# Another order of the work inside a turn: both later score tiles right behind the largest, two copies exchanged between the engines

## The chip, the cores and the metric

The kernel runs on one core of a Trainium2 chip. The core has four engines that compute, each with an instruction queue of its own: TensorE (PE in the profile, with its weight loads as PEld), VectorE (DVE), ScalarE (ACT) and GpSimd (POOL). SyncE (SP) and POOL issue the transfers. The engines wait for each other on semaphores. The metric is the device time of one execution in microseconds (us); the median of three runs of the kernel before is 439.67 us (438.95 to 440.5).

## The reference

Causal attention in blocks, and then a mixture of experts on its output:

```
scores = q @ k^T / 8            # 8 batches, 8 heads, 576 positions, 64 columns
scores = where(block(i) >= block(j), scores, -1e9)      # blocks of 64
attn   = exp(scores - max) / (sum + 1e-9);   x = attn @ v      # x: 4608 x 512
logits = x @ w_gate;  expert = argmax;  gate = softmax weight of that expert
for each of 8 experts: the 80 tokens of the highest gate
    out[tok] = gate * (relu(x[tok] @ w1[e]) @ w2[e])
```

All other rows of the output are zero.

## The kernel before, in words

Attention works on 32 pairs: pair i is batch i // 4 and two of its heads. For a pair, the 576 query rows are cut into five tiles. Tile u (0 to 3) has 128 rows, and because of the blocks its scores are (u + 1) * 128 + 64 columns wide: 192, 320, 448 and 576. Tile 4 is the first 64 rows, 64 columns. Each tile exists for both heads, h = 0 and 1. The steps of a pair, by their names in the table that orders them:

- `prep` 0 and 1: q and k, loaded in pieces, are turned by VectorE (L527); POOL scales the turned q (L530).
- `scores`: "3" makes tile 3 (a PSUM buffer for each head), "2" makes tiles 2 and 4 in one buffer, "10" makes tiles 1 and 0 in one buffer (L547, with the masking product L554).
- `max`: VectorE's negated maximum of each row (L583), for one head or for both.
- `soft`: ScalarE's exponential of a tile and head from PSUM into the array P, with the row's sum (L592).
- `back`: TensorE turns P in blocks of 64, "B" from tiles 1 and 2, "A" from tile 3, "C" the rest (L620, L628), each into one PSUM buffer.
- `take back`: a copy of that buffer to SBUF, A and B into PT, C into PF (L675 on ScalarE, L677 on VectorE; the dictionary TAKE says which).
- `values` 0 and 1: the product with v (L667, L646), from PT and PF into one PSUM buffer; `take values` copies it to xT, and `flip` turns it for the store (L294).
- `gate`: after the fourth pair of a batch, the parts of the routing: the sums' reciprocals (`recip`), the logits (`logits0`, their copy `lgc0` at L325, their turning `lt`, scaling `lm` at L351 and L360), the softmax (`ga`, `gexp`, `gb`), and its rearranging (`gturn`, `turn2`, `wcopy`).

All these PSUM buffers come from one pool of four (`ps_a`, L271), each of two banks, so that they hold the whole PSUM. A step that asks for a buffer gets one whose last reader stands earlier in the program, and waits for that reader. Five kinds of step ask: "3" for two, "2", "10", each `back` and `values` for one, and `logits0`, `lt` and `turn2` for one.

The order is written out by hand. In turn i (the loop at L702, from -5 to 37) the kernel goes through the table TURN; an entry (d, step, ...) does the step for pair i + d. No scheduler changes it: each engine gets its own instructions in the order in which the steps stand in the table. So TURN decides, for every engine, what stands in front of a waiting instruction, and for every PSUM buffer whom it waits for. A gate part of offset d falls into one turn of every four.

After the last pair come the selection of tokens and the experts' products, whose weights are streamed from HBM; this part has no line that the change touches.

Of the kernel before, what the change touches and what calls it, by code (L numbers as in the profile page):

```python
# [27 lines left out]

NVZ = 3

TAKE = {"back": {"A": "a", "B": "v", "C": "a"}, "values": {0: "a"}}

TWICE = (2,)

TURN = (
    (0, "scores", "3"),
    (-1, "take", "back", "C"),
    (0, "soft", 0, 1),
    (0, "max", 3, 1),
    (1, "begin"),  # L40
    (1, "scores", "2"),
    (0, "soft", 1, 0),
    (0, "soft", 0, 0),
    (0, "max", 3, 0),
    (1, "max", 2, 1),
    (0, "soft", 3, 1),
    (1, "max", 4),
    (1, "max", 2, 0),
    (-3, "gate", "ga"),
    (-1, "values", 0),  # L50
    (0, "soft", 3, 0),
    (0, "soft", 1, 1),
    (-1, "values", 1),
    (1, "soft", 2, 0),
    (-1, "gate", "recip"),
    (-5, "gate", "turn2"),
    (2, "prep", 0),
    (-2, "gate", "logits0"),
    (-5, "gate", "wcopy"),
    (0, "back", "B"),  # L60
    (1, "load_v"),
    (1, "soft", 4, 0),
    (-1, "take", "values", 0),
    (-4, "gate", "gb"),
    (1, "soft", 2, 1),
    (-2, "gate", "lgc0"),
    (1, "soft", 4, 1),
    (0, "back", "A"),
    (2, "prep", 1),
    (5, "load"),  # L70
    (-2, "gate", "lt"),
    (0, "take", "back", "B"),
    (1, "scores", "10"),
    (-4, "gate", "gturn"),
    (-2, "gate", "lm"),
    (0, "back", "C"),
    (1, "max", 0),
    (0, "take", "back", "A"),
    (1, "max", 1),
    (-2, "flip"),  # L80
    (-3, "gate", "gexp"),
)


# [1 line left out]
def tile_attn_moe(ctx, tc, q, k, v, w_gate, w1, w2, capacity, out, xs=None, dbg=None):  # L86
    nc = tc.nc
    B, H, S, D = q.shape
# [67 lines left out]
    def clear(i):  # L156
        if ov is not None:
            if 0 <= i < nz:
                nc.gpsimd.dma_start(ov[i], zero.unsqueeze(1).broadcast_to([P, 2, DM]))
        elif i == 0:  # L160
            for j in range(NTOK // BLK):
                nc.sync.dma_start(out[j * BLK:(j + 1) * BLK, :], zero[0:BLK, 0:DM])
# [30 lines left out]
    def constants():  # L193
        nc.gpsimd.memset(dl, 1e-9)
        nc.gpsimd.memset(zero, 0.0)
        nc.gpsimd.iota(iota_e, pattern=[[1, E]], base=-E, channel_multiplier=0,
                       allow_small_or_imprecise_dtypes=True)
        nc.gpsimd.iota(iota_v, pattern=[[0, NT], [1, E]], base=-E, channel_multiplier=0,
                       allow_small_or_imprecise_dtypes=True)
        nc.gpsimd.memset(iota_v[BLK:P, NT - 1], 64.0)  # L200
        nc.gpsimd.memset(prod[:, NT - 1], 0.0)

    def constants2():

        nc.vector.tensor_reduce(sameE, ident.rearrange("p (e j) -> p e j", j=16), axis=AX.X, op=ALU.add)
        nc.gpsimd.memset(sameR3, 0.0)
        nc.vector.tensor_reduce(sameR, ident.rearrange("p (e j) -> p j e", j=16), axis=AX.X, op=ALU.add)
        nc.gpsimd.tensor_copy(same.rearrange("p (e j) -> p e j", j=16), sameE.unsqueeze(2).broadcast_to([P, E, 16]))
        nc.gpsimd.memset(ones, 1.0)
        nc.gpsimd.iota(iota_s, pattern=[[1, CHUNK]], base=0, channel_multiplier=0,  # L210
                       allow_small_or_imprecise_dtypes=True)
        for i in range(2):
            nc.gpsimd.iota(iota_b[:, i], pattern=[[1 + i, CHUNK]], base=0, channel_multiplier=0,
                           allow_small_or_imprecise_dtypes=True)
        nc.gpsimd.iota(iota_p, pattern=[[0, 1]], base=0, channel_multiplier=1, allow_small_or_imprecise_dtypes=True)

        nc.gpsimd.affine_select(out=before, in_=same, compare_op=ALU.is_gt, fill=0.0, base=0,
                                pattern=[[1, P]], channel_multiplier=-1)
        nc.gpsimd.affine_select(out=after, in_=same, compare_op=ALU.is_gt, fill=0.0, base=0,
                                pattern=[[-1, P]], channel_multiplier=1)  # L220
        nc.gpsimd.tensor_tensor(before1, before, ident, op=ALU.add)
        nc.gpsimd.tensor_tensor(after1, after, ident, op=ALU.add)
        nc.gpsimd.iota(iota_c, pattern=[[1, 16]], base=0, channel_multiplier=0,
                       allow_small_or_imprecise_dtypes=True)

    def capacities():
        nc.vector.tensor_tensor(iota_c16, sameR, iota_c, op=ALU.mult)
        nc.vector.tensor_reduce(iota_r, iota_c16, axis=AX.X, op=ALU.add)
        nc.gpsimd.tensor_copy(cf, ci)
        nc.vector.scalar_tensor_tensor(cap, cf[:, 1:2], 4294967296.0, cf[:, 0:1], op0=ALU.mult, op1=ALU.add)  # L230
        nc.vector.tensor_tensor(caplt, iota_p, cap, op=ALU.is_lt)
# [41 lines left out]
    def banks():  # L273
        return ps_a.tile([P, 2, 512], F32, name="sc")
# [187 lines left out]
    class Pair:  # L462
# [209 lines left out]
        def take(self, what, x):  # L672

            if TAKE[what][x] == "a":
                nc.scalar.copy(*self.out.pop((what, x)))  # L675
# [3 lines left out]
    def warm(n, wt, after=None, w=identr, c=4):  # L679

        if not n:
            return
        with ExitStack() as order:
            if after is not None:
                order.enter_context(tc.issue_after(after.ins))
            for i in range(n):
                nc.tensor.matmul(wt[:, 0:c * P].rearrange("p (a c) -> p a c", c=P), lhsT=w,
                                 rhs=w.unsqueeze(1).broadcast_to([P, c, P]), start=(i == 0), stop=(i == n - 1))
# [9 lines left out]
    with tc.manual_schedule():  # L698
        warm(WARM[0], banks()[:, 0], w=idle)
        constants()  # L700
        constants2()
        for i in range(-5, n + 6):  # L702
            if i == -1:
                nc.sync.dma_start(ci, capacity.bitcast(U32).partition_broadcast(P))
                for h in range(2):
                    nc.sync.dma_start(wgd[h * D:(h + 1) * D, :, h * E:(h + 1) * E], wg_v[h])

            if i >= 4 and (i % 2 or i % 8 == 4) and i < n:
                clear(cleared)
                cleared += 1  # L710
            if i == 5:
                capacities()
            if n - 3 <= i < n - 3 + FW0:
                weights(1)
            for d, what, *args in (TURN if i != -1 else sorted(TURN, key=lambda x: x[1] == "prep")):
                j = i + d
                if not 0 <= j < n:
                    continue
                if what == "gate":
                    if j % NP == NP - 1 and j < n - 1:  # L720
                        batches[j // NP].part(args[0])
                    continue
                if what == "flip" and j >= n - NP:
                    continue
                getattr(pairs[j], what)(*args)
                if what == "flip" and j % NP == NP - 1:
                    batches[j // NP].done()
                if what == "take" and args[0] == "values" and j >= n - NP:
                    pairs[j].flip()
                    pairs[j].bt.store_pair(pairs[j].pr)  # L730
            if i == n:
                batches[B - 1].recip()
                batches[B - 1].store(False)
        while cleared < nz:
            clear(cleared)
            cleared += 1
        bt = batches[B - 1]
        for part in ((0, 384), (384, S)):
            bt.logits((part,))
            bt.lgc()  # L740
        bt.logits2(0, (3, NT))
        bt.logits2(1, (3, NT))
        bt.gate()
        bt.turn(nc.vector, 2)
        bt.turn2()
# [29 lines left out]
    key = sel.tile([P, 2, NH], F32, name="key")  # L775
# [503 lines left out]
```

## Time and profile before

| | us |
|---|---|
| median of three runs | 439.67 (438.95 to 440.5) |
| the profiled execution's own time | 436.93 |
| its span, first to last instruction | 434.9 |
| the first `values` of the program start at | 22.49 |
| the last `values` of the last pair start at | 307.33 |

The profile's page gives the busy time of each engine, the span in 40 slices, and the costliest groups of instructions. A row of the timeline gives the start of a group of like instructions, its length, the engine, the line, what it writes and reads, how many there are, and in brackets how long the engine stood idle before it and what ended that. The length of a group of TensorE is modelled to the end of its last instruction; the next group can start before that.

### The profile page before, as it was taken

The numbers are of one execution on the slowest core, as the hardware profiler recorded it, in microseconds if no ns is written. First come the engines' busy times: TensorE is split into PE (matmuls) and PEld (weight loads), VectorE is DVE, ScalarE is ACT, GpSimd is POOL, SyncE is SP. The second block draws the span as 40 slices with busy tenths as digits, with TensorE's granted clock in tenths as the row PEclk, the third lists the DMA queues.
The fourth block names the chain that finished last, engine by engine and source line by source line (L and its number), as shares of the span: only waits on it lengthen the run. The fifth ranks groups of instructions, "written<-read, shape, count | busy, mean of one in ns | idle before, by whom it ended". The sixth has DMA issues, their size and how long they took to land. (4 is left out here: it accounts for less than half of the span.)

```text
span 434.9 us, 15422 instructions
## 1 busy us (share of the span) xinstructions
PE 378.2 (87%) x6322; PEld 311.3 (72%) x6322; DVE 282.8 (65%) x586; ACT 265.0 (61%) x797; POOL 180.2 (41%) x296
## 2 busy tenths in 40 slices
PE   8789989899899889999989899899684999998990
PEld 4467767677777777777767677767463999998890
DVE  5987878987887897788789789885552221111121
ACT  2987878887887887798798878878320211110000
POOL 6535554443664445366344636562146400000010
PEclk9999999999999999999999999999988899999996
DMA  8999999989999898999989989399979999998920
GB/s 139 147 154 134 190 193 169 190 159 147 210 187 179 168 182 159 160 204 190 170 174 174 170 154 203 130 300 347 355 138 280 296 310 327 325 316 304 316 93 21
DMA packets 203836, 88.78 MB, mean 204 GB/s; under 512 B 168701, under 2 KB 185853, under 8 KB 203760
## 3 DMA queue, kind: packets, MB, share of 16 engines
q1 hardware_dynamic: 190112, 53.37, 63.0%
q0 software_dynamic: 12448, 34.07, 27.5%
q8 instruction: 52, 0.85, 0.9%
q10 hardware_dynamic: 1200, 0.30, 0.3%
q14 instruction: 24, 0.20, 0.2%
HBM read 67.58 MB, written 20.33 MB: 202 GB/s over the span
## 5 line engine op out<-in xcount | busy, mean ns | idle before, releaser
L592 ACT ACTIVATE P<-sc,negm 128x448 f32<-128x448 f32 (+2 forms) x320 | 163.7, 525 | 6.0 <-DVE negm L583 4.1
L583 DVE TENSOR_REDUCE negm<-sc 128x1 f32<-128x448 f32 (+4 forms) x224 | 125.7, 616 | 6.1 <-PE sc L554 6.0
L547 PE MATMUL sc<-T,T 64*128 64x64 f32 (+4 forms) x768 | 117.4, 413 | 3.0 <-POOL T L530 2.1
L547 PEld LDWEIGHTS sc<-T,T 64*128 64x128 f32 x768 | 84.0, 187 | 26.9 <-issue 7.2
L530 POOL TENSOR_SCALAR T<-T 128x576 f32<-128x576 f32 x31 | 20.5, 662 | 134.8 <-DVE T L527 114.1
L592 ACT ACTIVATION_READ_ACCUMULATOR P<-sc,negm 128x1 f32 x320 | 64.6, 202 | 0.0
L667 PE MATMUL sc<-PT,vn 128*64 128x128 f32 (+1 forms) x512 | 62.8, 379 | 0.0
L677 DVE COPY PT<-sc 128x1024 f32<-128x1024 f32 x32 | 38.8, 1213 | 28.9 <-ACT lgT L325 16.0
L667 PE MATMUL sc<-PF,vn 128*64 128x128 f32 x256 | 30.7, 282 | 29.1 <-ACT P L592 23.7
L667 PEld LDWEIGHTS sc<-PT,vn 128*64 128x64 f32 x512 | 43.8, 137 | 14.9 <-issue 1.4
L620 PE MATMUL sc<-ident,P 64*128 64x64 f32 x1280 | 52.3, 225 | 1.1 <-ACT P L592 1.0
L620 PEld LDWEIGHTS sc<-ident,P 64*128 64x128 f32 x1280 | 44.9, 139 | 5.9 <-ACT P L592 1.8
L527 DVE STREAM_TRANSPOSE T<-ld 128x576 f32<-128x576 f32 x62 | 45.2, 750 | 0.0
L507 POOL DMA_DIRECT2D vz<-in_v_dram x64 | 43.6, 694 | 0.0
L667 PEld LDWEIGHTS sc<-PF,vn 128*64 128x64 f32 x256 | 18.6, 136 | 33.7 <-ACT P L592 32.1
L986 PE MATMUL ps<-xsT,w 128*64 128x80 f32 x1024 | 40.7, 240 | 1.9 <-issue 1.9
L986 PEld LDWEIGHTS ps<-xsT,w 128*64 128x64 f32 x1024 | 38.5, 142 | 3.3 <-issue 2.4
L675 ACT COPY xT<-sc 128x576 f32<-128x576 f32 x32 | 20.5, 640 | 33.4 <-PE sc L646 33.4
L503 POOL DMA_DIRECT2D vn<-in_v_dram x64 | 40.1, 633 | 1.1 <-DMA w<-in_moe_w_dram 0.5
L1034 POOL DMA_INDIRECT out_dram<-y,si x8 | 7.4, 930 | 76.6 <-DVE y L1030 76.6
L675 ACT COPY PF<-sc 128x832 f32<-128x832 f32 x32 | 27.3, 853 | 13.7 <-PE sc L628 13.5
L1011 ACT ACTIVATE hT<-ps 128x320 f32<-128x320 f32 x16 | 7.0, 437 | 44.3 <-PE ps L986 44.3
(181 smaller groups left out, 500.5 us busy)
## 6 DMA issues: line engine op xcount, KB each, us to landing
w<-in_moe_w_dram SPq DMA_DIRECT2D x48, 512.0 KB, 5.1
out_dram<-zero POOLq DMA_DIRECT2D x18, 512.0 KB, 5.9
ld<-in_q_dram SPq DMA_DIRECT2D x124, 72.0 KB, 4.3
ld<-in_k_dram SPq DMA_DIRECT2D x124, 72.0 KB, 4.9
w<-in_moe_w_dram POOLq DMA_DIRECT2D x4, 2048.0 KB, 11.2
xs<-Y SPq DMA_DIRECT2D x28, 288.0 KB, 5.3
vz<-in_v_dram POOLq DMA_DIRECT2D x64, 80.0 KB, 5.1
vn<-in_v_dram POOLq DMA_DIRECT2D x32, 128.0 KB, 4.4
```

The lines of the kernel that those rows point to most:

```text
L503: nc.gpsimd.dma_start(self.vn[c * BLK:(c + 1) * BLK, 1], turned[:, :, 1 - c])
L507: nc.gpsimd.dma_start(self.vz[h * BLK:(h + 1) * BLK, h], even)
L527: nc.vector.transpose(t, self.nat[x].rearrange("p g d -> p (g d)"))
L530: nc.gpsimd.tensor_scalar(t, t, scalar1=SCALE, scalar2=1.0, op0=ALU.mult, op1=ALU.mult)
L547: nc.tensor.matmul(to[h], lhsT=self.T[0][r, q:q + P], rhs=self.T[1][r, k0:k1], start=start, stop=stop)
L583: nc.vector.tensor_reduce(to, src, axis=AX.X, op=ALU.max, negate=True)
L592: nc.scalar.activation(dst, src, AF.Exp, bias=self.negm[0:n, u, h:h + 1], scale=1.0, accum_out=self.bt.sums[0:n, u, self.h0 + h:self.h0 + ...
L620: nc.tensor.transpose(pt[:, c, to(c, n_)], row[u][r, h, k(u, h, j):k(u, h, j) + P], ident[r, r])
L667: nc.tensor.matmul(to, lhsT=lhs, rhs=rhs, start=(n_ == 0), stop=(n_ == len(steps) - 1))
L675: nc.scalar.copy(*self.out.pop((what, x)))
L677: nc.vector.tensor_copy(*self.out.pop((what, x)))
L986: yield nc.tensor.matmul(dst(b)[64 * c:64 * (c + 1)], lhsT=w_[:, a, col:col + 64], rhs=x_[:, a], start=(a == 0 and b == 0), stop=(a == n - ...
```

## The change

The table TURN is written in another order, some gate parts move to another turn, and two copies change their engine (TAKE): back B goes from VectorE to ScalarE, the values from ScalarE to VectorE. In the new table `scores "10"` is made for pair i (it was pair i + 1, at the end of the turn before), and stands right behind "3" and "2"; back C of pair i is done at the head of turn i + 1 (it stood at the end of turn i). The last line keeps, for the one turn of the start that puts `prep` last, only the prep of pair i + 2 there.

```
-TAKE = {"back": {"A": "a", "B": "v", "C": "a"}, "values": {0: "a"}}
+TAKE = {"back": {"A": "a", "B": "a", "C": "a"}, "values": {0: "v"}}
 TURN = (
     (0, "scores", "3"),
...
+    (-1, "back", "C"),
...
     (1, "scores", "2"),
+    (-1, "take", "back", "C"),
+    (0, "scores", "10"),
...
-    (1, "scores", "10"),
...
-            for d, what, *args in (TURN if i != -1 else sorted(TURN, key=lambda x: x[1] == "prep")):
+            for d, what, *args in (TURN if i != -1 else sorted(TURN, key=lambda x: x[:2] == (2, "prep"))):
```

On TensorE, in a turn without gate parts in the middle of the program; 512 columns are tile 3, 448 tile 2, 320 tile 1, 192 tile 0, and `ident` marks a `back`. Before:

```order
L667 MATMUL sc<-PF,vn 64x128 x2
...
L620 MATMUL sc<-ident,P_0_130 128x64 x16
L547 MATMUL sc<-T_1701,T_1642 128x320 x2
L547 MATMUL sc<-T_1701,T_1642 128x192 x2
...
L628 MATMUL sc<-ident,P_0_130 128x64
...
L547 MATMUL sc<-T_1701,T_1642 128x512 x2
...
L547 MATMUL sc<-T_1859,T_1811 128x448 x2
...
L667 MATMUL sc<-PF,vn 64x128 x2
```

Now, from one `values` to the next:

```order
L667 MATMUL sc<-PF,vn 64x128 x2
...
L620 MATMUL sc<-ident,P_0_130 128x64 x16
L547 MATMUL sc<-T_1701,T_1654 128x512 x2
...
L628 MATMUL sc<-ident,P_0_130 128x64
...
L547 MATMUL sc<-T_1859,T_1812 128x448 x2
...
L547 MATMUL sc<-T_1701,T_1654 128x320 x2
L547 MATMUL sc<-T_1701,T_1654 128x192 x2
...
L667 MATMUL sc<-PF,vn 64x128 x2
```

The pair's tiles 1 and 0 have moved from ahead of its tile 3 to behind the next pair's tile 2, directly in front of the `values`, and back C (L628) from ahead of tile 3 to behind it.

On ScalarE, a turn of the same stretch; P_0_126 to P_0_131 are the exponentials of tiles 0, 1, 2, 3 and 4. Before:

```order
L675 COPY PF<-sc 128x832
L592 ACTIVATE P_0_126,sums<-sc,negm 128x3x64
L592 ACTIVATE P_0_127,sums<-sc,negm 128x320
L592 ACTIVATE P_0_126,sums<-sc,negm 128x192
L592 ACTIVATE P_0_130,sums<-sc,negm 128x9x64
L592 ACTIVATE P_0_130,sums<-sc,negm 128x576
L592 ACTIVATE P_0_127,sums<-sc,negm 128x5x64
L592 ACTIVATE P_1_129,sums<-sc,negm 128x448
L592 ACTIVATE P_1_132,sums<-sc,negm 64x64
L675 COPY xT<-sc 128x576
L592 ACTIVATE P_1_129,sums<-sc,negm 128x7x64
L592 ACTIVATE P_1_132,sums<-sc,negm 64x64
```

Now:

```order
L675 COPY PT<-sc 128x4x2x128
L675 COPY PT<-sc 128x16x64
L675 COPY PF<-sc 128x832
L592 ACTIVATE P_0_130,sums<-sc,negm 128x9x64
L592 ACTIVATE P_0_130,sums<-sc,negm 128x576
L592 ACTIVATE P_1_129,sums<-sc,negm 128x7x64
L592 ACTIVATE P_1_129,sums<-sc,negm 128x448
L592 ACTIVATE P_0_126,sums<-sc,negm 128x3x64
L592 ACTIVATE P_0_127,sums<-sc,negm 128x320
L592 ACTIVATE P_0_127,sums<-sc,negm 128x5x64
L592 ACTIVATE P_1_132,sums<-sc,negm 64x64 x2
L592 ACTIVATE P_0_126,sums<-sc,negm 128x192
```

The three copies now stand together, tile 3 comes first of the exponentials, tiles 0 and 1 come behind tile 2 of the next pair, and the copy to xT has left ScalarE.

## Rows read from the trace of the kernel before

**Rows 1.** The page: the span.

```profile
span 434.9 us, 15422 instructions
```

**Rows 2.** The stretches view, mid-attention: busy time and count per engine, TensorE clock, DMA share, GB/s.

```profile
185.00:225.00 40.00, 36.46 (x562) 29.58 (x560) 33.78 (x61) 33.65 (x102) 21.35 (x34) 1.00 0.95 182
```

**Rows 3.** Waits from 60 to 300 us: total, times, longest.

```profile
PE sc L667 <- ACT P L592: 20.3, 22, 1.1
```

**Rows 4.** Timeline of TensorE: where the values of a pair start.

```profile
22.49 0.51 PE L667 MATMUL sc<-PF,vn 128*64 128x128 f32 x4 [0.76 <-ACT P L592]
...
190.25 0.51 PE L667 MATMUL sc<-PF,vn 128*64 128x128 f32 x4 [0.87 <-ACT P L592]
199.04 0.51 PE L667 MATMUL sc<-PF,vn 128*64 128x128 f32 x4 [0.87 <-ACT P L592]
...
208.10 0.51 PE L667 MATMUL sc<-PF,vn 128*64 128x128 f32 x4 [0.88 <-DMA vz<-in_v_dram]
...
218.88 0.51 PE L667 MATMUL sc<-PF,vn 128*64 128x128 f32 x4 [0.92 <-ACT P L592]
...
294.15 0.51 PE L667 MATMUL sc<-PF,vn 128*64 128x128 f32 x4 [1.10 <-ACT P L592]
...
307.33 0.51 PE L667 MATMUL sc<-PF,vn 128*64 128x128 f32 x4 [1.36 <-ACT PF L675]
```

**Rows 5.** Timeline of TensorE between the values at 190.25 and 199.04.

```profile
193.22 1.21 PE L620 MATMUL sc<-ident,P 64*128 64x64 f32 x32
...
194.26 1.08 PE L547 MATMUL sc<-T,T 64*128 64x320 f32 x8
...
195.24 0.41 PE L620 MATMUL sc<-ident,P 64*128 64x64 f32 x8
...
196.98 1.16 PE L547 MATMUL sc<-T,T 64*128 64x448 f32 x7
```

**Rows 6.** Timeline of ScalarE in the same turn.

```profile
188.45 0.52 ACT L592 ACTIVATE P<-sc,negm 128x320 f32<-128x320 f32 x1
...
188.96 0.42 ACT L592 ACTIVATE P<-sc,negm 128x192 f32<-128x192 f32 x1
...
189.37 0.74 ACT L592 ACTIVATE P<-sc,negm 128x576 f32<-128x576 f32 x1
...
190.10 0.73 ACT L592 ACTIVATE P<-sc,negm 128x576 f32<-128x576 f32 x1
...
193.32 0.64 ACT L675 COPY xT<-sc 128x576 f32<-128x576 f32 x1 [1.00 <-PE sc L646]
...
193.86 0.64 ACT L592 ACTIVATE P<-sc,negm 128x448 f32<-128x448 f32 x1
...
194.48 0.30 ACT L592 ACTIVATE P<-sc,negm 64x64 f32<-64x64 f32 x1
...
194.77 1.00 ACT L675 COPY PT<-sc 128x1024 f32<-128x1024 f32 x1
...
195.94 0.85 ACT L675 COPY PF<-sc 128x832 f32<-128x832 f32 x1 [0.17 <-PE sc L628]
```

**Rows 7.** Timeline of VectorE in the same turn.

```profile
188.56 2.64 DVE L583 TENSOR_REDUCE negm<-sc 128x1 f32<-128x576 f32 x5
...
193.97 1.23 DVE L677 COPY PT<-sc 128x1024 f32<-128x1024 f32 x1 [0.19 <-PE sc L620]
...
195.44 1.29 DVE L583 TENSOR_REDUCE negm<-sc 128x2 f32<-128x384 f32 x2 [0.25 <-PE sc L554]
```

**Rows 8.** Timeline of VectorE: the gate part `gb`, first instruction and the one behind it.

```profile
229.22 0.15 DVE L384 SCALAR_TENSOR_TENSOR eq<-lg,iota_e 128x40 f32<-128x40 f32 x1
...
230.51 0.78 DVE L527 STREAM_TRANSPOSE T<-ld 128x576 f32<-128x576 f32 x1
```

**Rows 9.** Timeline of VectorE: the gate part `lm`, and what follows it.

```profile
251.82 0.72 DVE L351 TENSOR_TENSOR prod<-sc,rs 128x256 f32<-128x256 f32 x2
...
252.98 1.28 DVE L583 TENSOR_REDUCE negm<-sc 128x2 f32<-128x384 f32 x2
```

More of the change, by code (lines that the diff above doesn't have):

```diff
@@ L36 @@
     (0, "scores", "3"),
-    (-1, "take", "back", "C"),
-    (0, "soft", 0, 1),
+    (-1, "back", "C"),
+    (-3, "flip"),
+    (-4, "gate", "gexp"),
     (0, "max", 3, 1),
+    (-2, "gate", "recip"),
+    (0, "max", 3, 0),
     (1, "begin"),
     (1, "scores", "2"),
-    (0, "soft", 1, 0),
-    (0, "soft", 0, 0),
[L44 to L59, printed above, removed]
+    (-1, "take", "back", "C"),
+    (0, "scores", "10"),
+    (1, "max", 2, 1),
+    (1, "max", 2, 0),
+    (0, "soft", 3, 1),
+    (0, "soft", 3, 0),
+    (1, "soft", 2, 1),
+    (-2, "gate", "logits0"),
+    (-5, "gate", "turn2"),
+    (0, "max", 0),
+    (0, "max", 1),
+    (-3, "gate", "lt"),
+    (-3, "gate", "lm"),
+    (-1, "values", 0),
+    (1, "soft", 2, 0),
+    (0, "soft", 0, 1),
+    (0, "soft", 1, 0),
+    (-1, "values", 1),
+    (-2, "gate", "lgc0"),
+    (-4, "gate", "gb"),
+    (-3, "gate", "ga"),
+    (1, "max", 4),
+    (0, "soft", 1, 1),
+    (1, "soft", 4, 1),
+    (-5, "gate", "wcopy"),
+    (2, "prep", 0),
+    (1, "soft", 4, 0),
+    (0, "soft", 0, 0),
     (0, "back", "B"),
     (1, "load_v"),
-    (1, "soft", 4, 0),
+    (-4, "gate", "gturn"),
+    (0, "back", "A"),
     (-1, "take", "values", 0),
[L64 to L68, printed above, removed]
     (2, "prep", 1),
     (5, "load"),
-    (-2, "gate", "lt"),
     (0, "take", "back", "B"),
-    (1, "scores", "10"),
[L74 to L77, printed above, removed]
     (0, "take", "back", "A"),
-    (1, "max", 1),
-    (-2, "flip"),
-    (-3, "gate", "gexp"),
 )
```

## The prediction

> **What bounds the kernel now.** I read the page first: the span is 434.9 us [rows 1], and its slices show attention on three quarters of it, with TensorE, ScalarE and VectorE all at 7 to 9 tenths. Then the stretches view: in the middle of attention TensorE is busy 36.46 of 40 us, ScalarE 33.65, VectorE 33.78 [rows 2]. TensorE leads, but it isn't full. The waits say what it waits for: ScalarE's exponentials, in front of the values, once a turn (the largest entry for TensorE) [rows 3]. The timeline gives the size: 0.87 us in front of each set of values [rows 4].
>
> A batch takes four turns of three lengths [rows 4]: 199.04 - 190.25 = 8.79 (two of them), 208.10 - 199.04 = 9.06 (with `turn2`), 218.88 - 208.10 = 10.78 (with the logits and their turning): 37.42 us.
>
> Why 8.79? Start where the values start, at 190.25, which is 0.15 after ScalarE began the instruction behind the first 576-wide exponential (190.10) [rows 4, 6]: that one was the wait. The values take 193.22 - 190.25 = 2.97, back B and A 1.04, tiles 1 and 0 0.98 [rows 5]; VectorE begins their maxima 0.20 later and takes 1.29 [rows 7]; ScalarE starts about 0.10 behind (an estimate: the chip shows such a gap at each hand-over) and does 192, 320, 192 and 576 columns, 0.41 + 0.51 + 0.41 + 0.73, start to start [rows 6], and 0.15 to the next values. The sum is 2.97 + 1.04 + 0.98 + 0.20 + 1.29 + 0.10 + 2.06 + 0.15 = 8.79. The turn is this loop: nothing in it can overlap, because tile 3's exponential waits on ScalarE behind those of tiles 0 and 1, whose scores stand on TensorE behind the values. TensorE's own work in a turn is 8.79 - 0.87 = 7.92.
>
> **The change: the new loop.** I walk through a turn without gate parts in the new order, from time 0, the start of tile 4's last exponential. Steps on ScalarE from start to start [rows 6]: 64 columns 0.29, 192 0.41, 320 0.51, 448 0.62, 576 0.73; a copy counts its length less the 0.10 by which the next instruction overlaps it (0.64 against 193.86 - 193.32 = 0.54): 0.90 for 1024 columns, 0.75 for 832. TensorE hands to ScalarE 0.28 after its last issue: back C issues from 195.24 on, its 13 of the 32 transposes that take 1.04 are 0.42, and the copy starts at 195.94 [rows 5, 6]. Tile 3 is then 196.98 - 195.66 = 1.32, tile 2 (the 7.92 less the other parts) 1.18.
> - TensorE: back A can start at 0.29 + 0.15 = 0.44 and takes 0.52; tile 3 to 2.28; back C to 2.70.
> - ScalarE meanwhile: tile 0's last exponential to 0.70, copy B to 1.60, copy A to 2.50. B is copied at about 1.75, before C's transposes want its buffer, A at 2.65, 0.05 before tile 2's scores want theirs at 2.70. The copy of C waits for C: 2.98 to 3.73. That idle half microsecond is the new wait.
> - TensorE: the next pair's tile 2 to 3.88; tiles 1 and 0, which need C's buffer (3.88), to 4.86; values 4.86 to 7.83, their buffer free at 4.61. The old wait is gone.
> - VectorE: tile 3's two maxima from 2.48; five reduces take 2.64 [rows 7], of which tile 2's have 896 of the 2176 columns, 1.09, and tile 3's some 1.4. Tile 2's run from 4.08 to 5.17; tiles 0 and 1's to 6.46.
> - ScalarE: tile 3's exponentials to 5.19; tile 2's wait for both maxima, 5.27 to 6.51; tiles 0 and 1 from 6.56, 1.43, to 7.99; tile 4's first to 8.28, where the last one starts: the loop is closed.
>
> So 8.28, and the gain 0.51 a turn. TensorE's stall is now 0.36, split by back B and A, which wait for the last exponentials. What the sum charges to nothing: copy B, 0.90 more on ScalarE, lies in the time in which ScalarE would wait for back C anyway. If it took VectorE's 1.23 [rows 7] tile 2 would come 0.2 late and the turn be 8.5; that is the upper bound, and the lower is A's own 1.00; I take A's, the same engine and size. The values' copy on VectorE isn't in the trace at 576 columns: between ScalarE's 0.64 and the 1.23 for 1024, say 0.70. VectorE loses 1.23 and gains 0.70. It ends some 0.6 before the next tile 3 wants its buffer. In a turn with many gate parts it ends with it, and I add 0.1 for those. Tile 4's maximum, which must now wait until tile 2's exponentials are done, has 1 us to spare. The POOL queue's v loads start about 1 us later in the turn, two turns ahead of their use; the q and k loads stand at the same place.
>
> **Gate parts.** Before, they cost 9.06 + 10.78 - 2 x 8.79 = 2.26 a batch. Now they are spread over four turns. TensorE's parts (logits, turning, `turn2`) fill its stall or push it only where ScalarE is late too. ScalarE's copy of the logits, of the shape of the one to xT, costs its 0.54. On VectorE `lm` is 252.98 - 251.82 = 1.16 [rows 9], `ga` behind it two small instructions, about 0.4; together they end at 6.46 + 1.56, so that tile 4's maximum (0.27) is done 0.4 late. `gb`, 230.51 - 229.22 = 1.29 [rows 8], comes 0.1 late. The reciprocals, two instructions and less than `gb`'s six, stand between tile 3's maxima and delay tile 2's, 0.4. Sum 1.5 and 0.2 for the two tight turns: the batch is 4 x 8.28 + 1.7 = 34.8 against 37.42, bounded by 33.1 (all gates hidden) and 36 (a gate costs what it did, and copy B its upper bound).
>
> **The sum.** From the first values to those 29 turns later the profile shows 294.15 - 22.49 = 271.7 [rows 4]. New: four turns without gates, 33.1, six batches, 208.8, and a turn with the logits' copy and the reciprocals, 9.2: 251.1, gain 20.6. Against it the ends: at the start tiles 1 and 0 of the first pair stand behind tile 2 of the second, which waits for that pair's `prep`; by the walk the first values come about 2 later (0 to 4). At the end the last two turns took 307.33 - 294.15 = 13.2 [rows 4], less than two turns, because no next pair is there; the new order has copy B, copy A and copy C between the last `back` and the last values, and by the walk takes 15.3. Net 20.6 - 2 - 2.1 = 16.5, and I take 16 for what the walk rounds away. What follows attention is the same work and starts that much earlier.
>
> The profiled execution took 436.93, which becomes 421. The median of the runs is 439.67, 2.7 more than the profiled one; 439.67 - 16 gives 424 for the median.
>
> **Rivals.**
> - *Half of it is lost to near ties.* The walk has copy A, tile 2's maxima, tiles 0 and 1's maxima and copy C each within 0.1 us of being the last. If two are late by 0.1 to 0.15 a turn, 8 of the 16 go: 432. For it: so many ties. Against: the same method gives the old turn to 0.01.
> - *VectorE holds the next tile 3.* One of tile 3's two buffers was the values'; their copy now stands on VectorE behind a `prep`, which needs its loads. VectorE is as busy as ScalarE [rows 2]; if each values copy came 0.5 late, 30 x 0.5 = 15 goes, and the time is 439. Against: VectorE's turn gets 0.5 shorter.
> - *The loads become the bound, and it gets slower.* The DMA engines' share is 0.95 in mid-attention [rows 2]. If no more than that can be had, the batch stays at 37.42 however the engines are ordered, while the ends still cost 4: 444. It decides from the point where the batch would fall below 37.4. Against: no row among the waits of VectorE shows it waiting for q or k, and a share that is counted from packets in flight isn't a limit by itself. The Trainium skill (DMA: Bandwidth & Descriptors, Specifications) says that transfers under 512 B don't reach line rate, and q and k come in pieces of 32 floats. By that rule the engines would be slow at their load rather than idle, the batch could not shrink, and the time would be that of this rival; the trace here shows the share, and no wait that bears it out.
> - *More than forecast.* The gate parts hide and the start costs nothing: 34.0 a batch and 2 less at the start gives 417.
> - *The order isn't what the engines do.* The instructions of an engine run as they stand in its queue, so this can only be a buffer that waits for another reader than I think; it would end near no change.
>
> **Chances.** Forecast 424, with its own range 419 to 429: 0.60. Ties, 429 to 436: 0.16. More than forecast: 0.07. VectorE holding tile 3, or another wait that takes the gain, around 439: 0.08. Loads, slower: 0.09. A measurement here tells 0.3%, 1.3 us, from no change: faster 0.60 + 0.16 + 0.07 and a part of the fourth, 0.86; the same 0.05; slower 0.09. The range that holds 8 in 10 is the forecast, the ties and part of the third: 418 to 436.
>
> **What would show it.** In the profile after: turns of about 8.3, 8.3, 8.7 and 9.2 us between the values; no idle time of TensorE before them; on ScalarE an idle half microsecond before the copy of C, ended by TensorE, in place of 1.00 before the copy to xT [rows 6]; idle time of TensorE moved to the second half of back B and to back A, ended by ScalarE; the first values at 24 to 25. Wrong would be: TensorE idle before tile 3 with VectorE's copy as the releaser (the second rival), VectorE's transposes waiting for DMA (the third), or a plain turn above 8.6 with waits of ScalarE for the maxima (the first).

## The result and the profile after

The changed kernel takes 424.94 us (median of four runs, 423.43 to 426.01); the kernel before took 439.53 beside it. The ratio is 0.9663, with a 95% interval of 0.9628 to 0.9698: 14.6 us faster. The forecast was 424. Its parts did not all come out so: attention won more than forecast in the middle and less at its start, and 4 us were lost behind attention.

The profiled execution took 424.61 us, against 436.93 before; that is 12.3 less, since the one before was 2.6 under its own median and this one 0.3. The page's span, against [rows 1]:

```profile
span 422.8 us, 15424 instructions
```

The stretches view, first for the same stretch as [rows 2], then for the first 25 us (span, then busy time and count of PE, PEld, DVE, ACT, POOL, the granted clock, the DMA share, GB/s):

```profile
185.00:225.00 40.00, 39.36 (x612) 29.61 (x610) 34.98 (x69) 37.97 (x112) 23.45 (x36) 1.00 1.01 205
...
0.00:25.00 25.00, 17.12 (x117) 10.09 (x119) 13.72 (x39) 11.46 (x33) 12.36 (x37) 0.80 1.03 138
```

TensorE is now busy 39.36 of 40 us, where it was 36.46; a short wait inside a group of like instructions counts as busy in this view. The waits from 60 to 280 us: the entry of [rows 3] is gone, and the wait of ScalarE that the prediction put in its place is small:

```profile
ACT PF L675 <- PE sc L628: 4.1, 19, 0.2
```

Where the values start, as [rows 4]; no idle time stands in front of them any more, except at the last:

```profile
27.14 0.44 PE L667 MATMUL sc<-PF,vn 128*64 128x128 f32 x4
...
43.35 0.44 PE L667 MATMUL sc<-PF,vn 128*64 128x128 f32 x4
...
51.49 0.44 PE L667 MATMUL sc<-PF,vn 128*64 128x128 f32 x4
...
62.08 1.18 PE L319 MATMUL sc<-xT,wgd 128*32 128x512 f32 x16 [2.37 <-ACT P L592]
...
63.22 0.51 PE L667 MATMUL sc<-PF,vn 128*64 128x128 f32 x4
...
200.99 0.44 PE L667 MATMUL sc<-PF,vn 128*64 128x128 f32 x4
...
209.51 0.44 PE L667 MATMUL sc<-PF,vn 128*64 128x128 f32 x4
...
217.38 0.44 PE L667 MATMUL sc<-PF,vn 128*64 128x128 f32 x4
...
226.00 0.44 PE L667 MATMUL sc<-PF,vn 128*64 128x128 f32 x4
...
234.93 0.44 PE L667 MATMUL sc<-PF,vn 128*64 128x128 f32 x4
...
277.41 0.44 PE L667 MATMUL sc<-PF,vn 128*64 128x128 f32 x4
...
290.73 0.51 PE L667 MATMUL sc<-PF,vn 128*64 128x128 f32 x4 [1.50 <-ACT PF L675]
```

A batch is 234.93 - 200.99 = 33.94 us (turns of 8.52, 7.87, 8.62, 8.93), where it was 37.42. One turn with no gate part in it is 51.49 - 43.35 = 8.14. In that turn, TensorE and then ScalarE (answering to [rows 5] and [rows 6]):

```profile
46.25 1.55 PE L620 MATMUL sc<-ident,P 64*128 64x64 f32 x32
47.63 1.25 PE L547 MATMUL sc<-T,T 64*128 64x512 f32 x8
...
48.74 0.44 PE L620 MATMUL sc<-ident,P 64*128 64x64 f32 x8
...
49.33 1.19 PE L547 MATMUL sc<-T,T 64*128 64x448 f32 x8
```

```profile
46.63 0.31 ACT L592 ACTIVATE P<-sc,negm 64x64 f32<-64x64 f32 x1
...
47.31 1.92 ACT L675 COPY PT<-sc 128x1024 f32<-128x1024 f32 x2
49.47 0.85 ACT L675 COPY PF<-sc 128x832 f32<-128x832 f32 x1 [0.24 <-PE sc L628]
50.22 0.75 ACT L592 ACTIVATE P<-sc,negm 128x576 f32<-128x576 f32 x1
...
54.76 0.32 ACT L592 ACTIVATE P<-sc,negm 64x64 f32<-64x64 f32 x1
```

ScalarE goes round once in 54.76 - 46.63 = 8.13 us with one short wait, the one for TensorE's back C: this round is the turn. Tile 3's scores issue in 48.74 - 47.63 = 1.11. The 32 transposes of back B and A take 47.63 - 46.25 = 1.38 to issue, where they took 1.04 before [rows 5]: TensorE's stall has moved to them, as the walk had it, and is 0.34 (forecast 0.36).

In the batch above, three of the four turns have no such stall; there TensorE, with the gate parts added, is the longer chain. In the turn from 209.51, for instance, the 32 transposes issue in 213.45 - 212.41 = 1.04:

```profile
212.41 1.21 PE L620 MATMUL sc<-ident,P 64*128 64x64 f32 x32
213.45 1.32 PE L547 MATMUL sc<-T,T 64*128 64x512 f32 x8
```

Three places lost time. The start: eight matmuls of 448 columns take 1.19 us at first and 2.18 after TensorE has stood idle for 3.42, and the granted clock of the first 25 us is 0.80 (1.00 before, in the same view): it fell from 2.4 to 1.2 GHz for a part of them.

```profile
8.42 1.19 PE L547 MATMUL sc<-T,T 64*128 64x448 f32 x8 [0.93 <-ACT T L522]
...
14.19 2.18 PE L547 MATMUL sc<-T,T 64*128 64x448 f32 x8 [3.42 <-POOL T L530]
```

Turn 5, 63.22 - 51.49 = 11.73 us. VectorE waits for a cast that stands on GpSimd behind the loads of v and a write of zeros, and ScalarE for the maxima behind it (its row names L289, the instruction right behind the maximum of tile 3):

```profile
59.42 0.16 DVE L230 SCALAR_TENSOR_TENSOR cap<-cf 128x1 f32<-128x1 f32 x1 [3.21 <-POOL cf L229]
```

```profile
61.20 0.74 ACT L592 ACTIVATE P<-sc,negm 128x576 f32<-128x576 f32 x1 [2.73 <-DVE rs L289]
```

And the end. GpSimd's first gather of tokens needs all stores of attention's output; before, then after:

```profile
328.26 1.14 POOL L877 DMA_INDIRECT xg<-xs,none  x1 [2.20 <-issue]
```

```profile
314.55 1.14 POOL L877 DMA_INDIRECT xg<-xs,none  x1 [5.03 <-DMA w<-in_moe_w_dram]
```

The last values come 307.33 - 290.73 = 16.6 us earlier than before, the gather only 13.7, the end of the span 12.1. The second row names a weight load, but the gather follows the stores: SyncE is done issuing the last one at 325.41 before the change and at 310.55 after it, 2.9 and 4.0 us ahead of the gather. The stretches view from 275 to 285 us, before and after, shows a lull of the DMA engines (share 0.43) that the faster attention no longer leaves (1.07); nor is it there earlier, for the shares in the 5 us stretches from 255 to 275 are 0.96 and more.

```profile
275.00:285.00 10.00, 9.11 (x146) 7.45 (x144) 8.49 (x16) 8.51 (x28) 5.57 (x9) 1.00 0.43 122
```

```profile
275.00:285.00 10.00, 10.00 (x142) 7.45 (x140) 8.65 (x18) 9.49 (x28) 6.70 (x11) 1.00 1.07 320
```

### The profile page after: what moved, and what is told of

The parts are those of the page before. It is cut to its first block, busy times and chain, and to the rows that moved or that the text cites. A ratio compares the mean times of both kernels' runs of the same rounds, so it can differ in the third digit from the quotient of the medians.

```text
span 422.8 us, 15424 instructions
## 1 busy us (share of the span) xinstructions
PE 381.9 (90%) x6322; PEld 297.9 (70%) x6322; DVE 269.9 (64%) x586; ACT 276.0 (65%) x797; POOL 179.8 (43%) x296
## 4 chain that ended last, share of the span: by engine, by line
PE 62%; POOL 8%; DVE 8%; DMA 7%; ACT 6%; issue 3%; SPq 3%; POOLq 0%; ACTq 0%; DVEq 0%
PE sc L547 14%; PE sc L667 13%; PE ps L986 11%; PE av L986 8%; PE sc L620 7%; ACT P L592 5%; DVE negm L583 3%; SPq L493 3%; POOL vz L507 2%; POOL vn L503 2%; PE sc L319 2%; DMA xs<-rs 1%; DMA xg<-xs,gi 1%; DMA ld<-in_k_dram 1%; POOL vn L500 1%
## 5 line engine op out<-in xcount | busy, mean ns | idle before, releaser
L592 ACT ACTIVATE P<-sc,negm 128x448 f32<-128x448 f32 (+4 forms) x320 | 164.0, 527 | 14.4 <-DVE negm L583 10.1
L547 PE MATMUL sc<-T,T 64*128 64x64 f32 (+4 forms) x768 | 112.7, 422 | 4.3 <-POOL T L530 3.4
L547 PEld LDWEIGHTS sc<-T,T 64*128 64x128 f32 x768 | 71.8, 191 | 34.7 <-issue 25.2
L592 ACT ACTIVATION_READ_ACCUMULATOR P<-sc,negm 128x1 f32 (+1 forms) x320 | 65.7, 205 | 0.0
L675 ACT COPY PT<-sc 128x1024 f32<-128x1024 f32 x64 | 61.6, 1018 | 1.9 <-PE sc L620 1.6
L620 PE MATMUL sc<-ident,P 64*128 64x64 f32 x1280 | 56.8, 230 | 3.7 <-ACT P L592 2.5
L667 PEld LDWEIGHTS sc<-PT,vn 128*64 128x64 f32 x512 | 34.8, 137 | 21.8 <-issue 20.4
L677 DVE COPY xT<-sc 128x576 f32<-128x576 f32 x32 | 23.7, 740 | 19.9 <-PE sc L646 19.9
L986 PE MATMUL av<-hT,w 128*64 128x80 f32 x896 | 32.9, 233 | 0.2 <-issue 0.2
L986 PEld LDWEIGHTS av<-hT,w 128*64 128x64 f32 x896 | 31.6, 137 | 1.5 <-issue 1.5
```

The lines of the kernel that those rows point to most:

```text
L547: nc.tensor.matmul(to[h], lhsT=self.T[0][r, q:q + P], rhs=self.T[1][r, k0:k1], start=start, stop=stop)
L592: nc.scalar.activation(dst, src, AF.Exp, bias=self.negm[0:n, u, h:h + 1], scale=1.0, accum_out=self.bt.sums[0:n, u, self.h0 + h:self.h0 + ...
L620: nc.tensor.transpose(pt[:, c, to(c, n_)], row[u][r, h, k(u, h, j):k(u, h, j) + P], ident[r, r])
L667: nc.tensor.matmul(to, lhsT=lhs, rhs=rhs, start=(n_ == 0), stop=(n_ == len(steps) - 1))
L677: nc.vector.tensor_copy(*self.out.pop((what, x)))
L986: yield nc.tensor.matmul(dst(b)[64 * c:64 * (c + 1)], lhsT=w_[:, a, col:col + 64], rhs=x_[:, a], start=(a == 0 and b == 0), stop=(a == n - ...
```

## The experiments

Each run has a ratio to the kernel before on the same chip; the changed kernel's is 0.9663.

### The parts of the change, one by one

**The new order with the old copies.**

```
-TAKE = {"back": {"A": "a", "B": "a", "C": "a"}, "values": {0: "v"}}
+TAKE = {"back": {"A": "a", "B": "v", "C": "a"}, "values": {0: "a"}}
```

> The new order, with the two copies back on their old engines (back B by VectorE, the values by ScalarE). Theory 1, the order: the gain of 14.6 us comes from the scores' place, which breaks the loop exponentials, values, scores, maxima, exponentials; the exchange is worth only what VectorE gets longer by, 1.23 - 0.74 = 0.5 us a turn at most, partly covered. Expected: 426 to 434 us, plain turns of 7.9 to 8.4 us, no idle time of TensorE in front of the values. Theory 2, the copies: the gain comes from the lighter VectorE and the values' buffer that comes free earlier. Expected: 436 us or more, with turns of 8.5 and longer.

Measured: 431.01 us, 0.9833 (0.979 to 0.9877), inside what I expected for the order. In the new order the exchange is worth 1.7%, about 7.5 us. A turn without gate parts is 52.24 - 43.74 = 8.50, as the prediction had it for copy B on VectorE, though not within the 7.9 to 8.4 expected here. No run moves one of the two copies alone, or the gate parts alone. ScalarE then waits for back C, whose transposes stand on TensorE behind VectorE's copy:

```profile
ACT PF L675 <- PE sc L628: 21.9, 24, 1.0
```

**The old order with the new copies.** The same line, in the kernel before, the other way round.

> The old order, with the exchange of the two copies alone. Theory 1, the order: none of the eight terms of the old turn's 8.79 us is one of the two copies, so the turn stays at 8.7 to 8.9 and the time at 437 to 443 us, with the idle 0.87 us in front of the values still there. Theory 2, the copies: 425 to 432 us, the idle time in front of the values gone.

Measured: 441.38 us, 1.0051 (1.002 to 1.0082). As expected for the order: the turn stays at 8.81, and the wait in front of the values stays. The exchange by itself gains nothing; it costs a little.

```profile
PE sc L667 <- ACT P L592: 17.7, 21, 0.9
```

**The old order with tiles 1 and 0 moved.**

```
     (1, "scores", "2"),
+    (0, "scores", "10"),
...
-    (1, "scores", "10"),
```

with the maxima of tiles 1 and 0 in front of the values and their four exponentials behind those of tile 3.

> The old order and the old copies, but tiles 1 and 0 of the pair itself right behind the next pair's tile 2 (they were the next pair's, at the end of the turn), with their maxima in front of the values and their exponentials behind those of tile 3; back C stays at the end of the turn, the gate parts where they were. Theory 1, the order: this one move breaks the loop; the turn falls towards TensorE's own 7.92 us, to 8.0 to 8.5, and the time is 426 to 433 us. Rival: the move works only with back C at the head of the next turn, and with the three copies together; then 436 us or more, and TensorE idle in front of back C or of tile 3.

Measured: 467.49 us, 1.0663 (1.0627 to 1.0699): 6.6% slower, and my expectation was wrong by some 35 us. Plain turns are 9.65. The waits from 60 to 280 us, with the timeline, say how: back C takes the buffer of the values (at 211.71 its transposes start, 0.05 behind the end of that copy), and the copy stands on ScalarE behind the exponentials of tiles 1 and 0 and the first ones of tiles 2 and 4; tile 3 stands behind back C, the maxima behind tile 3, and ScalarE waits for those.

```profile
ACT P L592 <- DVE negm L583: 34.5, 33, 1.6
...
PE sc L620 <- ACT xT L675: 12.9, 22, 0.7
```

One loop is cut, and a longer one that was covered by it is left. This move alone is not what gained.

**The new order with back C at the end of its own turn.**

```
-    (-1, "back", "C"),
...
     (0, "back", "A"),
+    (0, "back", "C"),
```

> The new order and the new copies, with back C again at the end of its own turn, right behind back A. Theory 1, the order of the scores alone: by the prediction's walk C's transposes start 0.96 us into the turn, when the last exponential of tile 0 (0.70) is done, so nothing waits; the time stays within 2 us of the changed kernel's 424.9. Rival: back C's place at the head of the next turn is needed, because TensorE must stand before C until the last exponentials are done; then 0.2 to 0.5 us a turn are lost, 430 to 440 us, with TensorE idle before L620 or L628, ended by ScalarE.

Measured: 435.13 us, 0.9924 (0.9891 to 0.9957). 2.6 of the gain's 3.4 points are gone, and I had expected none; the rival's time came, but not its wait. Gate-free turns are 8.62. TensorE doesn't wait for C's exponentials, in that the walk was right; but C's transposes now stand in front of tile 3, whose maxima are late, and ScalarE has nothing left to copy when it waits for them:

```profile
DVE negm L583 <- PE sc L554: 26.5, 24, 1.6
ACT P L592 <- DVE negm L583: 17.9, 53, 0.8
```

Behind tile 3, back C runs while VectorE makes the maxima, and its copy is done when they are.

### The three losses

**The capacity a turn later.** The part of this one-off computation that waits for the cast moves from turn 5 to turn 6.

```
             if i == 5:
                 capacities()
+            if i == 6:
+                capacities2()
```

> The changed kernel; of the capacity's small one-off computation in turn 5 the part of VectorE that waits for GpSimd's cast (L230, L231) is done a turn later, when the cast is long done. In the changed kernel VectorE stands 3.21 us before L230, because the cast stands on GpSimd behind the loads of v, and the maxima of tile 3 stand behind L230: that turn takes 11.73 us. Theory: VectorE's place at the head of the new turn made a wait that was free before decide; turn 5 falls to 8.9 to 9.4 us and the time by 2.0 to 2.8, to 422 to 423 us. Rival: the turn is long for its gate part (the logits) and the wait is only beside it; then the turn stays above 11 and the time within 0.6 us of 424.9.

Measured: 420.2 us, 0.9605 (0.9577 to 0.9633). Turn 5 falls from 11.73 to 60.35 - 51.09 = 9.26, the turn behind it from 9.19 to 8.53; against 0.9663 the ratio moves by 0.0058, some 2.5 us. As expected; the wait had cost the kernel before nothing (its L230 shows no idle time).

**The first pair ahead.** In turn 0 alone, the second pair's tile 2 with its maxima and exponentials goes behind the first pair's last exponential.

> The changed kernel; in turn 0 alone the second pair's tile 2, its maxima and exponentials stand behind the first pair's tiles 1 and 0 and all its exponentials. In the changed kernel TensorE stands 3.42 us from 10.77 on, for the second pair's turned q and k, and the clock then granted is half for some 9 us; the first values start at 27.14 instead of 22.49. Theory: the idle time and the clock that fell behind it are the loss of 4.65 us; the first values start at 22 to 24.5 us, the granted clock of the first 25 us is back to 0.9 or more, and the time falls by 2.5 to 4.5, to 420.5 to 422.5 us. Rival: the first turn is bound by ScalarE's exponentials and copies whatever the order; the first values stay at 26 to 27 and the time within 1 us of 424.9.

Measured: 422.51 us, 0.9666 (0.9636 to 0.9696): no change. The first values start at 26.46, and the clock stays at 0.80: TensorE stood 2.41 us, worked at 2.4 GHz, stood 2.19 more in front of back B, and was at half rate from there. The rival's numbers came; its reason isn't shown, since the clock fell here too.

**The start as before**, with the capacity's edit: in turn 0 tiles 1 and 0 ahead of tile 3, their maxima and exponentials too, then the second pair.

> The changed kernel with the capacity's wait a turn later, as in the run of that edit alone, and turn 0 in the old order of the start: the first pair's tiles 1 and 0 ahead of its tile 3, their maxima and exponentials too, and the second pair's tile 2 behind tile 3, its exponentials behind all of the first pair's. With only the second pair set back, the clock granted in the first 25 us stayed at 0.80, for TensorE now stood in front of back B (2.19 us). Theory: with back B's exponentials done first, TensorE has work from 13.7 to 20 us, as before the change; the clock of the first 25 us goes to 0.9 or more, the first values start at 22 to 24.5 us, and the time is 2.5 to 4.5 us under that of the capacity's edit alone (ratio to before 0.950 to 0.956 where that had 0.9605). Rival: what is won at the start is lost where the loads of q and k are late, in the turns behind it; the ratio stays above 0.958.

Measured: 420.78 us, 0.9586 (0.9548 to 0.9624), not told apart from 0.9605. First values at 27.14, clock 0.82. TensorE stands 2.44 and 1.78 us, with 1.2 of work between. The start's loss was not got back. How much of it is the clock and how much ScalarE's longer work ahead of the first values stays open; one comparison speaks against a large part of the clock. In the run of the capacity's edit alone, turn 0 is that of the changed kernel, but the clock of the first 25 us is 0.86, some 3 us less at half rate; the first values still start 26.72 - 7.88 = 18.84 behind the first scores, where the changed kernel has 27.14 - 8.42 = 18.72.

**The first weights at turns 22, 24, 26, 28.**

```
-            if n - 3 <= i < n - 3 + FW0:
+            if i in (22, 24, 26, 28):
```

> The changed kernel; the first four weight loads of 2 MB each, issued by GpSimd at turns 29 to 32, are issued at turns 22, 24, 26 and 28. Theory A: at the end of attention the transfers are behind; the stores of the last batch stand in SyncE's queue behind slow stores, and the gather of the tokens waits 5.03 us for them. With the weights earlier the gather's wait falls under 1.5 us, the last values stand where they are (within 1 us), and 2 to 4 us come back: 421 to 423 us. Theory B, the loads bind attention (the prediction's third rival): with 2 MB more in every second turn the turns 22 to 28 become longer by 0.5 us or more each, the last values come 3 us later or more, and the time is 425 to 430 us.

Measured: 439.88 us, 1.007 (1.0039 to 1.01). Theory B was right about attention, and more strongly than I priced it. Two turns took 18.55 and 19.18 us instead of 8.52, with VectorE waiting for q (waits, 220 to 300 us):

```profile
DVE T L527 <- DMA ld<-in_q_dram: 17.1, 2, 9.0
```

Theory A was right about the end: from the last values (311.9) to the end of the span are 123.6 us, against 132.1 in the changed kernel. Less was won there than attention lost.

**All three together.**

> The edits of the three other runs of this call together: the capacity's wait a turn later, the first pair ahead in turn 0, the first weights earlier. If the three losses stand one behind the other, as the theories say, the gains add: 415 to 419 us. If what is saved early is lost again at the end, to transfers that no longer have time to hide, the time is not below 420 us.

Measured: 435.6 us, 0.9969 (0.9944 to 0.9994). I had expected 415 to 419; the weights' loss in attention outweighs the rest.

**One weight load a batch**, at turns 14, 18, 22 and 26, with the capacity's edit.

> The changed kernel with the capacity's wait a turn later, and the first four weight loads issued at turns 14, 18, 22 and 26, one a batch and two turns or more from the stores of the batch before. With them at 22, 24, 26 and 28 two turns grew by 9 us, where VectorE waited for q behind the stores; the ones at 22 and 26 did no harm. Theory: the end of attention is then free of 8 MB of transfers, the gather waits less than 1.5 us for the last stores, and 2 to 4 us come back: ratio to before 0.951 to 0.956 (0.9605 without). Rival: attention has no room for 2 MB anywhere, and each load costs a turn some us: ratio 0.965 or more, VectorE waiting for q or k.

Measured: 441.84 us, 1.0052 (1.0017 to 1.0086). My expectation was wrong, and its rival nearer: the load at turn 14 lengthened no turn that it fell into, but each of the three others made one of 15.36 to 17.82 us where 7.87 were needed without it, VectorE waiting for k (waits, 60 to 280 us):

```profile
DVE T L528 <- DMA ld<-in_k_dram: 24.8, 6, 8.4
```

Attention had room for one load of 2 MB, not for four; why one does harm and another doesn't stays open.

**The same, with the zeros earlier.**

```
-            if i >= 4 and (i % 2 or i % 8 == 4) and i < n:
+            if 0 <= i < 27 and i % 3 != 2:
                 clear(cleared)
```

> As the run with one weight load a batch, and the 18 writes of zeros (512 KB each) in two of three turns from 0 to 26, in place of the turns 4 to 31. If the writes of zeros in the last turns still hold the last stores up, another 0.5 to 1.5 us come back, and the ratio to before is 0.948 to 0.954; if they hold nothing up, it stays within 0.002 of the run without this edit; if the early turns have no room, the turns 1 to 4 grow above 8.2 us.

Measured: 439.34 us, 0.9995 (0.9959 to 1.0031). The ratio expected (0.948 to 0.954) was out of reach with the weights' loss in it, and the interval overlaps that of the run before. Up to the first weight load in turn 14 its turns are like those of the capacity's edit alone but for one (9.06 for 8.61): the early turns have room for the zeros.

**The zeros earlier, the weights where they were**, with the capacity's edit.

> The changed kernel with the capacity's wait a turn later and the weights at their own turns (29 to 32), but the 18 writes of zeros (512 KB each) in two of three turns from 0 to 26, in place of the turns 4 to 31; four of them leave the turns 27 to 31. Theory: what the change lost behind attention are transfers that stand in front of the last stores; 2 MB fewer at some 350 GB/s are 6 us of transfers less there, the gather's wait of 4.34 us goes or halves, and the stretch from the last values to the end (131.2 us in the run without this edit, 127.6 before the change) falls to 127 to 129.5: ratio to before 0.951 to 0.957 (0.9605 without). Rival 1: attention has no room for them either, as for the weights; turns grow by some us, and the ratio is 0.961 or more. Rival 2: the last stores are slow by themselves (pieces of 128 bytes), not for what stands ahead; the stretch stays at 131 and the ratio within 0.002 of 0.9605.

Measured: 417.31 us, 0.9515 (0.9479 to 0.9552): the fastest version, 0.9% under that of the capacity alone, some 4 us, as expected. The gather waits 1.33 us in place of 4.34, and from the last values to the end are 415.3 - 286.16 = 129.1 us (131.2 without):

```profile
307.14 1.14 POOL L880 DMA_INDIRECT xg<-xs,none  x1 [1.33 <-issue]
```

From the last values to the gather are 20.98 us, as before the change (20.93; 23.37 without this edit). So what the change lost up to the gather was transfers in front of the last stores. Some 1.5 us behind the gather were not got back, and their cause is open.

A part of the gain lies elsewhere: the last values come 1.0 us earlier. The changed kernel has a long turn, from 148.15 to 157.63, in which TensorE waits for a gate part of GpSimd that stands behind the loads of v; GpSimd issued the first of them 0.83 us late, for nothing that the profile shows. Here that turn is 8.60 instead of 9.48. In the changed kernel:

```profile
157.35 0.35 PE L413 MATMUL sc<-sp,sameR 128*32 128x40 f32 x16 [1.00 <-POOL sp L400]
```

Of the second rival a part holds: SyncE still needs 10.32 us to issue the last twelve stores (9.11 without). The Trainium skill (DMA: Bandwidth & Descriptors, Specifications) says that transfers under 512 B don't reach line rate; these are pieces of 128 B, 864 KB in those 10.32 us, some 85 GB/s, while the ten us from 275 on move 324 GB/s. The trace fits that, though no run changed the pieces, and the issuing itself may be what takes the time.

## Why the prediction was right, and where it was wrong

- **The diagnosis held.** The idle 0.87 us in front of the values was what could be won, and it went. TensorE's own work was put at 7.92 a turn and the gate parts at 2.26 a batch: 4 x 7.92 + 2.26 = 33.94, and the batch measured 33.94. As much as all of the old wait, 4 x 0.87 = 3.48, is gone from each batch. That the two agree to the hundredth is chance: the 7.92 held a wait in tile 3 (next point), and the new turns have short waits of their own, such as the 0.34 in a plain turn.
- **The plain turn was 0.14 too long.** Forecast 8.28, measured 8.13 and 8.14. Walk and trace agree on ScalarE to 0.02 as far as the first copy (0.70 and 0.68) and again from tile 3's exponentials to the end (4.55 and 4.54). The step that failed is "Tile 3 is then 196.98 - 195.66 = 1.32": that difference of start times held a wait, and tile 3 issues in 1.11. Before the change its second buffer was back A's, whose copy ended at 194.77 + 1.00 = 195.77 [rows 6]; one of its matmuls issues at 195.55, the next at 195.82 (the rows below). So C came earlier, the copy of C at 2.84 for 2.98. The walk's idle half microsecond starts 0.10 before the end of the second copy; from that end, as the profile counts, it is 0.38, and less the 0.14 it is the measured 0.24. Before the change:

```profile
195.55 0.65 PE L547 MATMUL sc<-T,T 64*128 64x512 f32 x1
...
195.82 1.12 PE L547 MATMUL sc<-T,T 64*128 64x512 f32 x5
```

- **The gate parts were charged to the wrong chain.** The step "Sum 1.5 and 0.2 for the two tight turns" laid them on ScalarE's and VectorE's chain. In a turn with gate parts TensorE is the longer chain, and its wait of 0.36 takes them in (1.04 for back B and A, not 1.38). The batch is 33.94 for 34.8, inside the bounds of 33.1 and 36; of the 0.86, 4 x 0.14 = 0.56 is the plain turn, and the gate parts cost 33.94 - 4 x 8.14 = 1.38 where 1.7 was forecast.
- **The end of attention** cost nothing: the last two turns took 290.73 - 277.41 = 13.32, as before 13.18, where the walk had 15.3. The three copies do stand in front of the last values, as the walk said, but before the change three copies stood there too, with that to xT in the place of B's, and the wait for the last of them was 1.36 us [rows 4], 1.50 now. The walk had put the copies on top of it.
- **The start was outside its bounds.** First values at 27.14, forecast 24 to 25, bounds 0 to 4 for a loss that was 4.65. The step "by the walk the first values come about 2 later" knew the wait for `prep` (3.42 idle, 2.07 before), not that the clock would fall behind it, nor that TensorE would stand 2.50 more in front of back B for ScalarE's exponentials; no run shows what each of them cost.
- **Turn 5 wasn't seen.** The walk asked for every step of the table what stands behind it, but not for the one-off call in front of the table: 2.5 us.
- **"What follows attention is the same work and starts that much earlier" was false.** It is the same work on the engines, but its transfers were hidden by attention's length. Of a lead of 16.6, 4.5 went (3.6 with the capacity's edit, of which 2.1 came back with the zeros earlier).
- **Sum.** Over the 29 turns from the first values 277.41 - 27.14 = 250.3, forecast 251.1; the lead at the last values 16.6, forecast 16.5: the 29 turns gained 0.8 more than forecast, in spite of turn 5, the end 2.0 more, and the start 2.65 less. That these errors cancel is luck. The profiled time was 3.6 over its forecast of 421, for the loss behind attention. That the median's forecast was met to 1 us is in part luck: the profiled execution before was 2.6 under its median.
- **Rivals.** The ties did not take the 8 us of their rival. One was lost: copy A ends at 47.31 + 1.92 = 49.23 and tile 2's scores start at 49.33, where the walk had the copy done 0.05 ahead of them. VectorE's copy of the values held nothing. The loads did not bind attention, but stand at the edge of it: 2 MB more bound it by 7 us and more in five of the eight places tried in the two runs with the old zeros, and not in the three others. That rival had its mechanism right and its threshold too early. The changes are not additive: exchange alone +0.5%, order alone -1.7%, both -3.4%; a forecast from one part would have failed.

## What to carry to other kernels

Price a hand-written order as one loop through all engines, and take each step's length from its own row, not from the distance to the next one, which may hold a wait. When the middle of a kernel gets shorter, look at what was hidden under it: transfers that had a lull have none, and one-off waits that had slack decide. Moving a transfer works only to a place where the loads of the loop leave room, so try the small ones first.

## What the runs showed of the hardware

TensorE was granted half its clock after 3.42 us without work at the start, and also where it stood 2.41 and 2.19 us with 1.2 us of work between (first pair ahead); before the change 2.07 and 0.77 us of idling left it at 1.00. In the changed kernel a DMA share of 1.01 (185 to 225 us) and 1.07 (275 to 285) went with no wait of VectorE for q or k, and with four loads of 2 MB put into attention VectorE waited for q up to 9.0 us at a time: the share alone doesn't show how near the edge is.
